# LN(x) of the first layer: from normalized rows kept in DRAM to raw column quarters centred on the fly

## The chip, the cores and the metric

The kernel runs on one core of a Trainium2 chip. That core has a matrix engine (TensorE, PE in the profile), a vector engine (VectorE, DVE), a scalar engine (ScalarE, ACT), a general engine (GpSimd, POOL) and a queue engine that issues most of the transfers (SyncE, SP). Each engine works through its own list of instructions in order and waits for the others by semaphores. The metric is the device time of one execution in microseconds.

## The reference

Four layers act in turn on `x`, an array of 2048 positions by 512 channels. Layers one and three (A) and layers two and four (B) are a LayerNorm, a long causal convolution done by Fourier transforms, and a residual addition.

```python
def _layernorm(x, axis=-1, eps=1e-5):
    m = jnp.mean(x, axis=axis, keepdims=True)
    v = jnp.var(x, axis=axis, keepdims=True)
    return (x - m) / jnp.sqrt(v + eps)
...
    x = A_q
    x = x + _A_ref(_layernorm(x, axis=-1), A_k, A_v, A_shift_k, A_ssm_k, A_ssm_D)
    x = x + _B_ref(_layernorm(x, axis=-1), B_log_A_real, B_A_imag, B_C_real, B_C_imag, B_log_dt, B_D_skip)
...
```

`_A_ref(q, k, v, ...)` returns `q * y`, where `y` comes from `k`, `v` and the filter alone and does not depend on `x`. So the first layer is `x + LN(x) * y`, with `LN(x) = (x - mean) / std`. Both the kernel before and the changed one compute it without the mean, as `x - mean + LN(x) * y`, and keep the mean in a small tile `off` for later. `y` of layer A is stored (`ya_d`) and used again for layer three.

## The kernel before

**Stages.** The program has a planned stage, from about 25 to 550 us of the profiled execution, and then the rest in the order in which it is written: layer two, the update of layer three and layer four. The change touches the planned stage alone.

**What the planned stage holds.** Two generators are recorded side by side. `stream()` makes the taps of layer B's filter: 64 steps, four for each of 16 groups of channels. A step is an angle matmul into the PSUM tile `pa`, a rounding on VectorE (`y`), a second matmul, five sine or absolute-value activations on ScalarE (`ab`, `tt`, `pa`), two products on GpSimd (`xy`) and one on VectorE (`e2`), and 16 small matmuls (`pk`). Every fourth step scales `pk` into `ks`, which goes to DRAM (`kdram`), comes back as `kk`, and is transformed (`pf`, `zk`, `pu`, `pc`) into the filter's spectrum `spec1`. Each of the steps 0, 8, 16 and so on has a block of six exponentials (`m`) ahead of it. I call these 64 steps the taps.

`diagonal()` does layer A: the filter's spectrum (`spectrum_quarter(0, ...)`), the products `kv` of 16 channel groups (`gated`, with operand tile `kvt` and result `u`, eight elementwise operations shared by VectorE and GpSimd), and the convolution for four quarters of 128 channels. The convolution goes by pairs of chunks: `pu` by matmul, a copy `sw` on ScalarE, the products `sw` on GpSimd and `vv` on VectorE with the loaded spectrum `kab`, then the inverse transform `pi` (64 small matmuls a pair), copied back to `zu` by ScalarE, transposed to `w`, and multiplied into `po`. `po` has one PSUM buffer. `finish_a` copies it to `ya` and calls `update_a`, which writes the new `x` of 32 channels.

**Where LN(x) comes from.** `row_stats` loads the 16 blocks of rows of `x` (`xt`, 256 KB each in two transfers) and takes their statistics. `normalizer` turns them into `rs` (1/std), `nm` (minus the mean) and `nb`, at tap 32 (`XN`). `ln_rows(j)` then loads four blocks of rows (`xr`, 1 MB), normalizes each on ScalarE, and writes the result by channel quarter to `ln_d` (16 transfers in all). `load_x(q)` reads a quarter back as `xq`, a single buffer of 1 MB. `update_a` multiplies: `po + std`, then `xq * po`. When a quarter is done it is stored to `x1_d`, and only then can the next quarter be loaded into the buffer.

**What sets the order.** Nothing in the planned stage is issued as it is recorded. `Planner.plan` simulates the recorded operations with a cost for each (`Planner.cost`) and places, again and again, the operation that could start earliest; each engine's list is the result. A transfer is planned to land at the later of 1500 ns after its issue and 1200 ns after a common server, moving 290 bytes a nanosecond, has moved its size. The order so found is fixed: on the chip an engine waits at the head of its list even when later work is ready. SyncE's list is one of these lists: a store that waits for its data holds back the loads behind it. Since all places follow from the costs, a change of cost moves instructions all over the stage.

**Lines.** The profile gives planned instructions the line 319, where the planner emits them, and the others 177; tiles tell them apart.

Of the kernel before, what the change touches and what calls it, by code (L numbers as in the profile page):

```python
# [9 lines left out]
F32 = mybir.dt.float32  # L10
# [10 lines left out]
NQ = 4  # L21
# [87 lines left out]
class Planner:  # L109
# [70 lines left out]
    def cost(self, op):  # L180
        name, a, k = op.calls[0]
        aps = [x for x in list(a) + list(k.values()) if hasattr(x, "tensor")]
        free = lambda x: int(np.prod([c for _, c in x.ap[1:]])) if len(x.ap) > 1 else 1
        n = max(free(x) for x in aps)
        if name == "dma_start":
            size = 4 * n * max(1, aps[0].ap[0][1]) if aps[0].space != DRAM else 4 * int(np.prod([c for _, c in aps[0].ap]))
            return (450 if op.engine == "D" else 600), 1500 + size / 290, size
        big = [x for x in aps[1:] if free(x) > 1]
        psum = [x.space == PSUM for x in big]
        if op.engine == "T":  # L190
            total, each = 0, 0
            for _, b, _ in op.calls:
                d = free(b[2]) * (1 if b[2].dtype == F32R else 4) / 2.4
                area = b[1].ap[0][1] * free(b[1]) / 16384
                total, each = total + d * area, max(each, d)
            return max(total, each), max(total, each) + 230, 0
        if op.engine == "V":
            alone = len(big) == 1 and not psum[0] and name in ("tensor_copy", "tensor_scalar", "tensor_scalar_mul")
            o = 60 + n * (0.52 if alone else 1.06)
            return o, o + 85, len(big) > 1 and not any(psum)  # L200
        if op.engine == "S":
            o = n / 1.2 + (50 if all(psum) else 184)
            if any(hasattr(k.get(x), "tensor") for x in ("scale", "bias")):
                o = n / 1.2 + (186 if name == "activation" and len(big) == 1 else 280)
            return o, o + 105, 0
        o = 100 + 2.2 * n if name.startswith("tensor_tensor") or name in ("tensor_mul", "tensor_add", "tensor_sub") else 100 + 0.9 * n
        return o, o + 50, n > 1
# [123 lines left out]
def kernel(ctx: ExitStack, tc: tile.TileContext, out, x_in, kv_in, ssmk_in, ssmd_in,  # L331
# [13 lines left out]
    ya_d = dram.tile([4, 128, 16, 128], F32, name="ya_d")  # L345
    kv_d = [dram.tile([128, 512], F32, name=f"kv_d{g}") for g in range(16)]

    ln_d = [dram.tile([128, 16, 128], F32, name=f"ln_d{q}") for q in range(NQ)]
    x1_d = [dram.tile([128, 16, 128], F32, name=f"x1_d{q}") for q in range(NQ)]
    rows_d = [dram.tile([NQ, 128, 4, 128], F32, name=f"rows_d{k}") for k in range(2)]  # L350

# [94 lines left out]


    off = cpool.tile([128, 16], F32, name="off")
    std = cpool.tile([128, 16], F32, name="std")
    st = cpool.tile([128, 16, 4, 6], F32, name="st")  # L450
    st_all = lambda t: st[:, t, :, :].rearrange("p q s -> p (q s)")

# [334 lines left out]
    def taps():  # L787
        load_rows(0)
        load_rows(1)

        def exps(gi):
            mags(gi, 0, 2)
            mags(gi, 0, 1)
            mags(gi, 1, 1)

        for n in range(64 + LP + LC):
            gi, k = divmod(n, 4)
            if n < 64:
                if k == 0:
                    if gi > 0 and gi < 15:  # L800
                        load_rows(gi + 1)
                    if EORD == 1:
                        exps(gi)
                    elif EORD == 3 and gi % 2 == 0:
                        exps(gi)
                        exps(gi + 1)
                if n == XN:
                    root = normalizer(0, 16, lambda t: st0[:, t, :])
                    after(root, last_exp[0])
                    last_exp[0] = root  # L810
                    V.reciprocal(std, rs)
                    G.tensor_scalar(off, nm, -1.0, None, op0=ALU.mult)
                angles(gi, k)
                waves(gi, k)
            if 0 <= n - LP < 64:
                products(*divmod(n - LP, 4))
            m = n - LP - LC
            if 0 <= m < 64:
                contract(*divmod(m, 4))
                if m % 16 == 15:  # L820
                    todo.append(spectrum_quarter(1, m // 16, kdram, kp, zlast_k, 1))
            yield
# [12 lines left out]
    with ExitStack() as actx:  # L835
# [29 lines left out]

        KV0 = 1
        KVE = 0b10010110
        def row_stats(t):
            xt = ap.tile([128, 512], F32, name="xt", tag="kk", bufs=NKK)
            by_half(xt, x_in[:, t, :])  # L870
            V.bn_stats(st0[:, t, :], xt)

        def kv_steps():
            for grp in range(KV0, 16):
# [21 lines left out]
            return (lambda: z[0]), [nop] * 7 + [lambda: load(0)] + [nop] * 4 + turns  # L896


        def ln_rows(j):
            xr = ap.tile([128, 4, 512], F32, name="xr", tag="xq", bufs=1)  # L900
            by_half(xr.rearrange("p t c -> p (t c)"), x_in[:, 4 * j:4 * j + 4, :].rearrange("p t c -> p (t c)"))
            for i in range(4):
                t = 4 * j + i
                S.activation(xr[:, i], xr[:, i], AF.Identity, scale=rs[:, t:t + 1], bias=nb[:, t:t + 1])
            for q in range(NQ):
                Q.dma_start(ln_d[q][:, 4 * j:4 * j + 4, :], xr[:, :, 128 * q:128 * q + 128])

        xqs = {}

        def load_x(q):  # L910
            xqs[q] = ap.tile([128, 16, 128], F32, name="xq", tag="xq", bufs=1)
            Q.dma_start(xqs[q], ln_d[q])


        def update_a(q, g, po):
            xs = xqs[q][:, :, 32 * g:32 * g + 32]
            ins = V.tensor_add(po, po, std[:, :, None].to_broadcast([128, 16, 32]))
            V.tensor_mul(xs, xs, po)

        def stats_a(q, c):  # L920
            if 3 <= c < 7:
# [11 lines left out]
        def diagonal():  # L933
            kvs = kv_steps()
            for q in range(NQ):
                for i, _ in enumerate(spectrum_quarter(0, q, ssmk_in, ap, zlast, ZA)):
                    if q == 0 and i == 1:
                        for grp in range(KV0):
                            for _ in gated(grp, 255):
                                pass  # L940
                    if q == 0 and i < 4:
                        Q.dma_start(w2[:, 8 * i:8 * i + 8], w2_in[:, 8 * i:8 * i + 8])
                    if q == 2 and i < 4:
                        ins = Q.dma_start(mm[:, 8 * i:8 * i + 8], mm_in[:, 8 * i:8 * i + 8])
                        after(ins, zlast[0])
                    if q == 3 and i == 0:
                        after(Q.dma_start(w4, w4_in), zlast[0])
                    next(kvs, 0)
                    if q == 3 or q == 2 and i >= 8:
                        row_stats(12 * (q - 2) + i - 8)  # L950
                    yield
            for _ in kvs:
                yield
            for s, _ in enumerate(convolution(0, {"conv": ap}, steps_a, finish_a, lag=LAGA, ahead=AHA, nk=NKA, ns=NSA,
                                              nw=NWA, inplace=True, zlast=zlast, late_step=stats_a), -2 * NCH):
                if s >= LN0 and (s - LN0) % LNS == 0 and s < LN0 + 4 * LNS:
                    ln_rows((s - LN0) // LNS)
                if s >= 0 and s % NCH == LX and s // NCH < NQ:
                    load_x(s // NCH)
                yield  # L960

        LN0, LNS = -8, 3
        LX = 7

        RT = 2
# [247 lines left out]
```

## Time and profile before

| | us |
|---|---|
| median of 3 runs (lowest, highest) | 798.61 (795.02, 799.39) |
| the profiled execution: its time | 799.61 |
| the profiled execution: first to last instruction (span) | 797.6 |
| planned stage, about | 25 to 550 |
| TensorE busy in the span | 551.8 |
| VectorE, ScalarE, GpSimd busy | 516.9, 432.9, 391.1 |
| mean granted TensorE clock | 0.783 of full speed |

The span is read from the trace of one execution; 2.0 us of that execution lie around it. Terms worked out from the trace are taken off or added to the execution's own 799.61 us, which is 1.0 us above the median of the runs. A busy share is an average; which engine ends a wait is read in each stretch, from the chain of waits and from the rows of the timeline.

### The profile page before, as it was taken

To read this page: it belongs to the slowest core of one execution; us is meant where nothing else is said; L and a number is where in the kernel's file an instruction comes from. 1 tells how busy PE (TensorE), PEld (TensorE's weight loads), DVE (VectorE), ACT (ScalarE), POOL (GpSimd) and SP (SyncE) were. 2 spreads that over 40 slices of the span, in tenths; PEclk is the share of its full clock that TensorE was granted. 3 is DMA by queue.
4 is the path that set the end of the run, shared out by engine and by line. 5 is a ranking of instruction groups with operands and counts; after the bars stand their busy time and mean duration, and the time that the engine had idled before them with its cause. 6 is when DMAs were issued, how large, how long until landed. Compare 5 with 4: busy or idle time off the path is not lost.

```text
span 797.6 us, 20671 instructions
## 1 busy us (share of the span) xinstructions
PE 551.8 (69%) x8440; PEld 321.3 (40%) x8440; DVE 516.9 (65%) x931; ACT 432.9 (54%) x800; POOL 391.1 (49%) x362
## 2 busy tenths in 40 slices
PE   1467665576568767697787588763499982669995
PEld 0134333234235333465335246432165560246562
DVE  6545555886864475354567654855368898987773
ACT  4066383284367786873862348813845343847441
POOL 3776768777756172663461315810064441245451
PEclk9995565575855567777659887977789997789998
DMA  8675756464855446758536773646878634047874
GB/s 242 205 177 135 228 168 180 115 174 141 227 149 180 161 129 187 214 174 250 202 98 192 220 271 126 201 139 228 254 261 292 219 133 145 14 134 251 257 223 92
DMA packets 77634, 147.33 MB, mean 185 GB/s; under 512 B 8668, under 2 KB 37732, under 8 KB 74980
## 3 DMA queue, kind: packets, MB, share of 16 engines
q1 hardware_dynamic: 76676, 143.60, 58.4%
q0 software_dynamic: 864, 2.43, 1.0%
q8 instruction: 66, 1.08, 0.6%
q14 instruction: 28, 0.23, 0.1%
HBM read 101.95 MB, written 44.04 MB: 183 GB/s over the span
## 4 chain that ended last, share of the span: by engine, by line
PE 36%; DVE 23%; ACT 17%; issue 9%; DMA 9%; POOL 4%; SPq 1%; DVEq 0%; ACTq 0%; POOLq 0%
PE pf L319 6%; PE pa L319 5%; PE pu L319 5%; PE pk L319 4%; ACT m L319 4%; PE pi L319 4%; PE pi L177 3%; DMA kab<-spec 3%; ACT tt L319 2%; PE pu L177 2%; PE po L319 2%; PE pf L177 2%; DVE zu L177 2%; DVE x L177 2%; DVE w L177 2%
## 5 line engine op out<-in xcount | busy, mean ns | idle before, releaser
L319 POOL TENSOR_TENSOR xy<-tt,m 128x512 f32<-128x512 f32 x128 | 151.6, 1205 | 98.5 <-ACT tt L319 55.2
L177 POOL TENSOR_TENSOR sw<-sw,kab 128x512 f32<-128x512 f32 x64 | 80.7, 1281 | 117.1 <-ACT sw L177 115.5
L319 PE MATMUL pf<-kk,w 64*128 64x512 f32 x128 | 62.7, 955 | 36.6 <-DMA kk<-ssmk_in 19.5
L319 ACT ACTIVATE m<-pm 128x1024 f32<-128x1024 f32 x48 | 47.1, 1023 | 67.6 <-PE pm L319 50.8
L319 PE MATMUL pk<-xy,e 128*32 128x64 f32 x2048 | 57.5, 274 | 17.4 <-POOL xy L319 13.6
L319 DVE STREAM_TRANSPOSE zk<-pf 128x512 f32<-128x512 f32 x64 | 42.1, 693 | 40.3 <-PE pf L319 40.2
L319 DVE TENSOR_TENSOR e<-pa,m 128x512 f32<-128x512 f32 x64 | 43.6, 683 | 35.4 <-ACT pa L319 25.3
L319 ACT ACTIVATE ab<-pa 128x512 f32<-128x512 f32 x64 | 38.2, 597 | 51.2 <-PE pa L319 50.5
L319 POOL TENSOR_TENSOR sw<-sw,kab 128x512 f32<-128x512 f32 x32 | 40.6, 1279 | 51.7 <-ACT sw L319 29.8
L319 PE MATMUL pa<-tt,rw 64*128 64x512 f32 x64 | 42.8, 672 | 32.3 <-DVE e L319 29.7
L177 DVE TENSOR_TENSOR vv<-pu,kab 128x512 f32<-128x512 f32 x64 | 41.2, 679 | 33.8 <-ACT sw L177 30.5
L177 ACT COPY ie<-pi 128x1024 f32<-128x1024 f32 x32 | 32.4, 1013 | 56.0 <-PE pi L177 54.5
L319 PEld LDWEIGHTS pk<-xy,e 128*32 128x32 f32 x2048 | 44.3, 143 | 43.7 <-POOL xy L319 28.1
L319 PE MATMUL pa<-y,minus 128*128 128x512 f32 x64 | 42.6, 671 | 26.2 <-DVE y L319 26.2
L319 DVE TENSOR_SCALAR y<-pa 128x512 fp32r<-128x512 f32 x64 | 43.6, 683 | 25.6 <-PE pa L319 25.5
L319 PE MATMUL pu<-zk,w 64*64 64x128 f32 x1024 | 50.7, 360 | 11.0 <-ACT pc L319 5.2
L319 POOL TENSOR_TENSOR u<-u,tb 128x512 f32<-128x512 f32 x32 | 44.4, 1390 | 23.4 <-DVE tb L319 12.7
L177 PE MATMUL pf<-u,w 64*128 64x512 f32 (+1 forms) x136 | 39.3, 665 | 23.3 <-ACT u L177 15.1
L177 PE MATMUL pi<-vv,mm 64*64 64x128 f32 x1024 | 53.6, 275 | 1.2 <-DVE vv L177 1.1
L177 PE MATMUL pi<-sw,mm 64*64 64x128 f32 x1024 | 52.8, 270 | 0.7 <-issue 0.7
L319 PEld LDWEIGHTS pu<-zk,w 64*64 64x64 f32 x1024 | 42.6, 185 | 26.0 <-issue 12.8
L319 ACT ACTIVATE tt<-pa 128x256 f32<-128x256 f32 x128 | 44.7, 387 | 10.9 <-PE pa L319 7.1
(141 smaller groups left out, 1264.8 us busy)
## 6 DMA issues: line engine op xcount, KB each, us to landing
kab<-spec SPq DMA_DIRECT2D x94, 512.0 KB, 5.4
spec<-pc SPq DMA_DIRECT2D x64, 256.0 KB, 2.2
kvt<-kv_in SPq DMA_DIRECT2D x32, 312.0 KB, 6.0
kk<-ssmk_in SPq DMA_DIRECT2D x32, 128.0 KB, 3.1
kv_d<-u SPq DMA_DIRECT2D x16, 256.0 KB, 4.0
xr<-x_in SPq DMA_DIRECT2D x8, 512.0 KB, 5.1
kdram<-ks SPq DMA_DIRECT2D x64, 64.0 KB, 1.8
kk<-kdram SPq DMA_DIRECT2D x32, 128.0 KB, 2.9
```

The costliest lines, as they stand in the source:

```text
L177: op.ins = getattr(self.engines[key], name)(*a, **k).ins
L319: ins = getattr(self.engines[op.engine], name)(*a, **k).ins
```

## The change

Three things change. `Planner.cost` counts a transfer at the size of its destination. Before, it multiplied the number of destination partitions by the longer of the two sides' free sizes, which counted every half-partition transfer (`by_half`: `kk`, `kvt`, `xr`, `xt`) and every broadcast `kab` load at twice its size.

`row_stats(j)` now loads `xr` (1 MB, four blocks) and takes the statistics from it, four times, in quarter 1 of the filter's spectrum (`LNQ`). `ln_rows` and `ln_d` are gone: no normalized row is written or read back.

`load_x(q)` reads the raw quarter of `x` in four transfers of 32 partitions each (256 KB, in pieces of 512 bytes), and GpSimd subtracts the mean (`off`) in four operations of 128x512. `update_a` becomes `po * rs`, then `(po + 1) * xq`: with `xq = x - mean` this is `x - mean + LN(x) * y` as before. `std` is gone.

```diff
@@ Planner.cost
         if name == "dma_start":
-            size = 4 * n * max(1, aps[0].ap[0][1]) if aps[0].space != DRAM else 4 * int(np.prod([c for _, c in aps[0].ap]))
+            size = 4 * int(np.prod([c for _, c in aps[0].ap]))
@@ taps
-                    V.reciprocal(std, rs)
                     G.tensor_scalar(off, nm, -1.0, None, op0=ALU.mult)
@@
-        def row_stats(t):
-            xt = ap.tile([128, 512], F32, name="xt", tag="kk", bufs=NKK)
-            by_half(xt, x_in[:, t, :])
-            V.bn_stats(st0[:, t, :], xt)
+        def row_stats(j):
+            xr = ap.tile([128, 4, 512], F32, name="xr", tag="xq", bufs=1)
+            by_half(xr.rearrange("p t c -> p (t c)"), x_in[:, 4 * j:4 * j + 4, :].rearrange("p t c -> p (t c)"))
+            for i in range(4):
+                V.bn_stats(st0[:, 4 * j + i, :], xr[:, i])
@@
-        def ln_rows(j):
-            xr = ap.tile([128, 4, 512], F32, name="xr", tag="xq", bufs=1)
-            by_half(xr.rearrange("p t c -> p (t c)"), x_in[:, 4 * j:4 * j + 4, :].rearrange("p t c -> p (t c)"))
-            for i in range(4):
-                t = 4 * j + i
-                S.activation(xr[:, i], xr[:, i], AF.Identity, scale=rs[:, t:t + 1], bias=nb[:, t:t + 1])
-            for q in range(NQ):
-                Q.dma_start(ln_d[q][:, 4 * j:4 * j + 4, :], xr[:, :, 128 * q:128 * q + 128])
@@
         def load_x(q):
             xqs[q] = ap.tile([128, 16, 128], F32, name="xq", tag="xq", bufs=1)
-            Q.dma_start(xqs[q], ln_d[q])
+            rows = x_in[:, :, 128 * q:128 * q + 128].rearrange("(a b n) t c -> a b n t c", a=2, b=2)
+            for b in range(2):
+                for a in range(2):
+                    Q.dma_start(xqs[q][64 * b + a:64 * b + 64:2], rows[a, b])
+            for j in range(4):
+                ts = slice(4 * j, 4 * j + 4)
+                G.tensor_sub(xqs[q][:, ts], xqs[q][:, ts], off[:, ts, None].to_broadcast([128, 4, 128]))
 
         def update_a(q, g, po):
             xs = xqs[q][:, :, 32 * g:32 * g + 32]
-            ins = V.tensor_add(po, po, std[:, :, None].to_broadcast([128, 16, 32]))
-            V.tensor_mul(xs, xs, po)
+            V.tensor_mul(po, po, rs[:, :, None].to_broadcast([128, 16, 32]))
+            V.scalar_tensor_tensor(xs, po, 1.0, xs, op0=ALU.add, op1=ALU.mult)
@@ diagonal
-                    if q == 3 or q == 2 and i >= 8:
-                        row_stats(12 * (q - 2) + i - 8)
+                    if q == LNQ and i % 3 == 0:
+                        row_stats(i // 3)
@@
-                if s >= LN0 and (s - LN0) % LNS == 0 and s < LN0 + 4 * LNS:
-                    ln_rows((s - LN0) // LNS)
                 if s >= 0 and s % NCH == LX and s // NCH < NQ:
                     load_x(s // NCH)
@@
-        LN0, LNS = -8, 3
+        LNQ = 1
         LX = 7
```

Because the costs change, the plan changes everywhere. Three places follow, with the instructions as the two programs list them; the number behind a name tells buffers of one name apart and differs between the programs.

First, SyncE's list around the fourth to seventh load of the convolution's spectrum (`kab`). Before:

```order
L319 DMA kab_771<-spec0_0_57 128x1x1024
L319 DMA raw_936<-rows_d1_107 128x128
L319 DMA kab_773<-spec0_0_57 128x1x1024
L319 DMA kab_790<-spec0_0_57 128x1x1024
L319 DMA ln_d0_98<-xr_734 128x4x128
L319 DMA ln_d1_99<-xr_734 128x4x128
L319 DMA ln_d2_100<-xr_734 128x4x128
L319 DMA ln_d3_101<-xr_734 128x4x128
L319 DMA spec1_1_62<-pc_783 128x512
L319 DMA spec1_1_62<-pc_789 128x512
L319 DMA kab_792<-spec0_0_57 128x1x1024
L319 DMA kab_799<-spec0_0_57 128x1x1024
```

and now:

```order
L319 DMA kab_751<-spec0_0_57 128x1x1024
L319 DMA raw_915<-rows_d1_103 128x128
L319 DMA kab_752<-spec0_0_57 128x1x1024
L319 DMA spec1_1_62<-pc_762 128x512
L319 DMA kab_769<-spec0_0_57 128x1x1024
L319 DMA spec1_1_62<-pc_768 128x512
L319 DMA kab_771<-spec0_0_57 128x1x1024
L319 DMA u_801<-kv_d7_89 128x512
L319 DMA kab_778<-spec0_0_57 128x1x1024
```

The stores of normalized rows, which wait for ScalarE's `xr`, no longer stand between the sixth and the seventh load.

Second, GpSimd's list in the convolution, around the tile `xy` of one tap and the products `sw`. Before:

```order
L319 TENSOR_TENSOR xy_941<-tt0_228,m1_865 128x16x32 x2
L319 TENSOR_TENSOR xy_949<-tt1_229,m1_869 128x16x32 x2
L319 TENSOR_TENSOR xy_981<-tt2_230,m1_871 128x16x32
L319 TENSOR_TENSOR kk_916<-kk_916,dr_879 1x4x8
L319 TENSOR_TENSOR xy_981<-tt2_230,m1_871 128x16x32
```

and now, where the same taps are `xy_920`, `xy_928` and `xy_960`:

```order
L319 TENSOR_TENSOR xy_920<-tt0_223,m1_844 128x16x32 x2
L319 TENSOR_TENSOR sw_912<-sw_912,kab_884 128x512
L319 TENSOR_TENSOR sw_912<-sw_912,kab_904 128x512
L319 TENSOR_TENSOR xy_928<-tt1_224,m1_848 128x16x32
L319 TENSOR_TENSOR xq_908<-xq_908,off_117 128x512 x4
L319 TENSOR_TENSOR xy_928<-tt1_224,m1_848 128x16x32
L319 TENSOR_TENSOR sw_935<-sw_935,kab_909 128x512
L319 TENSOR_TENSOR sw_935<-sw_935,kab_913 128x512
```

The four subtractions of the second quarter stand between the two halves of one tap's `xy`, and the convolution's products stand earlier among the taps. Those of the third quarter stand likewise inside a tap; the first quarter's are spread over a few taps, and the fourth's stand among the last `kk` additions.

Third, ScalarE's list at the end of the planned stage, from the last tap on. Before:

```order
L319 ACTIVATE ab_1101<-pa_1099 128x512
L319 ACTIVATE tt0_228<-pa_1099 128x8x32 x2
L319 ACTIVATE tt0_228<-ab_1101,halfpi_145 128x8x32
L319 ACTIVATE pa_1099<-pa_1099 128x8x32
L319 ACTIVATE pa_1099<-ab_1101,halfpi_145 128x8x32
L319 COPY zu_975<-pi_1092 128x64x16
L319 COPY zu_975<-pi_1104 128x64x16
L319 COPY ya_1108<-po_1107 128x512
```

and now:

```order
L319 COPY zu_954<-pi_1083 128x64x16
L319 ACTIVATE ab_1080<-pa_1078 128x512
L319 ACTIVATE tt0_223<-pa_1078 128x8x32 x2
L319 ACTIVATE tt0_223<-ab_1080,halfpi_140 128x8x32
L319 ACTIVATE pa_1078<-pa_1078 128x8x32
L319 ACTIVATE pa_1078<-ab_1080,halfpi_140 128x8x32
L319 COPY ya_1087<-po_1086 128x512
```

Both last copies of `pi` stood behind the last tap; now both stand ahead of it.

More of the change, by code (lines that the diff above doesn't have):

```diff
@@ L346 @@
     kv_d = [dram.tile([128, 512], F32, name=f"kv_d{g}") for g in range(16)]
-    ln_d = [dram.tile([128, 16, 128], F32, name=f"ln_d{q}") for q in range(NQ)]
     x1_d = [dram.tile([128, 16, 128], F32, name=f"x1_d{q}") for q in range(NQ)]
@@ L448 @@
     off = cpool.tile([128, 16], F32, name="off")
-    std = cpool.tile([128, 16], F32, name="std")
     st = cpool.tile([128, 16, 4, 6], F32, name="st")
```

## Prediction

> **What bounds the kernel now.** I read the summary of the page first, then the busy time by stretches, then the chain of waits in the planned stage, then the timeline of its end.
>
> ```profile
> span 797.6 us, 20671 instructions
> PE 551.8 (69%) x8440; PEld 321.3 (40%) x8440; DVE 516.9 (65%) x931; ACT 432.9 (54%) x800; POOL 391.1 (49%) x362
> ...
> PE 36%; DVE 23%; ACT 17%; issue 9%; DMA 9%; POOL 4%; SPq 1%; DVEq 0%; ACTq 0%; POOLq 0%
> ```
>
> No engine is full. The last line divides the chain that ended last: TensorE has a third, VectorE a quarter, ScalarE a sixth, transfers 9%, GpSimd 4%. So a microsecond taken from one engine is not a microsecond of time; it depends on the stretch.
>
> ```profile
> core 0: us, PE busy (x) PEld busy (x) DVE busy (x) ACT busy (x) POOL busy (x), PEclk, DMA share, GB/s
> 100.00:150.00 50.00, 26.82 (x332) 15.87 (x336) 30.58 (x38) 29.55 (x63) 37.09 (x30) 0.56 0.57 164
> 200.00:250.00 50.00, 33.03 (x425) 18.47 (x425) 34.77 (x58) 25.79 (x53) 33.57 (x30) 0.72 0.64 185
> 300.00:350.00 50.00, 38.47 (x576) 23.85 (x567) 21.56 (x35) 39.44 (x77) 23.81 (x22) 0.69 0.71 204
> 400.00:450.00 50.00, 40.63 (x663) 23.13 (x663) 34.79 (x63) 22.11 (x41) 21.63 (x22) 0.80 0.58 177
> 500.00:550.00 50.00, 35.06 (x594) 20.25 (x594) 36.47 (x77) 21.30 (x42) 18.02 (x18) 0.86 0.55 179
> ```
>
> Up to 250 us GpSimd is the busiest or close to it. From 300 to 350, where `ln_rows` runs, ScalarE is (39 of 50 us) and the transfers are heaviest. From 400 on TensorE and VectorE lead, and GpSimd works under half the time. The change takes ScalarE work and transfers out of the third of these stretches and puts most of its GpSimd work where GpSimd is half idle.
>
> **Part by part.** The sum is made against the profiled execution, 799.6 us.
>
> *(a) The normalization on ScalarE goes.* Sixteen instructions:
>
> ```profile
> L319 ACT ACTIVATE xr<-xr,nb,rs 128x512 f32<-128x512 f32 x16 | 11.7, 801 | 1.6 <-DMA xr<-x_in 1.0 <-DVE nb L319 0.6
> ```
>
> They come in four blocks of 2.9 us. Only one is on the chain:
>
> ```profile
> 335.47 4.61 DMA kab<-spec
> 340.08 0.66 ACT xr L319
> 340.77 2.21 ACT xr L319 x3
> ...
> 347.91 3.48 DMA kab<-spec
> ...
> 359.30 7.42 DMA u<-kv_d
> ```
>
> 0.66 + 2.21 = 2.9. Bounds: 0 (all hidden) and -11.7 (all exposed). I take -2.9, what the chain shows.
>
> *(b) `ln_d`, its queue time and 8 MB of traffic go.* Rows of `x` were read twice (4 + 4 MB), LN(x) written and read (4 + 4); now they are read twice. The chain rows above hold 4.61 + 3.48 + 7.42 = 15.5 us of waits for loads that stand behind `xr` and `ln_d` on SyncE, and SyncE waited for ScalarE's rows:
>
> ```profile
> SPq L319 <- ACT xr L319: 13.8, 3, 6.9
> POOL sw L319 <- DMA kab<-spec: 3.4, 4, 1.3
> ```
>
> The first row: 13.8 us in three waits, at the head of the list, with `kab`, `spec` and `u` behind. In the new list nothing of this kind stands between the `kab` loads. But a load takes its time on a free queue too (the 5.4 us below), so not all of 15.5 can go. Bounds 0 and -15.5; I take about half, -7.
>
> *(c) The end of the stage is shorter.* Rounding of the last tap, then what followed it:
>
> ```profile
> 511.44 0.69 DVE L319 TENSOR_SCALAR y<-pa 128x512 fp32r<-128x512 f32 x1 [0.51 <-PE pa L319]
> 512.61 0.45 PE L319 MATMUL pi<-vv,mm 64*64 64x128 f32 x8
> 514.20 0.34 SPq L319 DMA_DIRECT2D x_d<-xq  x1
> 519.07 0.34 SPq L319 DMA_DIRECT2D xq<-ln_d  x1
> 524.91 2.43 PE L319 MATMUL pf<-kk,w 64*128 64x512 f32 x8
> 531.92 0.69 DVE L319 TENSOR_TENSOR xq<-xq,po 128x512 f32<-128x512 f32 x1
> ...
> 554.01 6.60 DMA x<-x_d
> ```
>
> Two `pi` pairs lie between the tap and the first `pf` (512.61 to 524.91, 12.3 us). In the new lists both precede the last tap; they have to fit into gaps further ahead. Bounds 0 (they displace other work) and -12.3; I take -5.
>
> *(d) Sixteen subtractions on GpSimd come in.* The nearest row, two 128x512 operands on the same engine:
>
> ```profile
> L319 POOL TENSOR_TENSOR sw<-sw,kab 128x512 f32<-128x512 f32 x32 | 40.6, 1279 | 51.7 <-ACT sw L319 29.8 <-DMA spec<-pc 17.7 <-DMA kab<-spec 3.4
> ```
>
> 16 x 1.28 = 20.5 us. Twelve come in three clumps of four, 5.1 us each. Behind a clump wait half an `xy` (then `pk`, `ks`, `kdram`) and the `sw` products. GpSimd was idle 51.7 us ahead of this group alone, so most is covered. Bounds 0 and +20.5; I take one clump exposed, +5.1. Without its cover the whole 20.5 is paid.
>
> *(e) The turnaround of `xq`.* Before, 519.07 to 531.92 lay between the issue of the last quarter's load and its first use, 12.9 us. Now there are four issues on SyncE and then the clump.
>
> ```profile
> kab<-spec SPq DMA_DIRECT2D x94, 512.0 KB, 5.4
> xr<-x_in SPq DMA_DIRECT2D x8, 512.0 KB, 5.1
> ln_d<-xr SPq DMA_DIRECT2D x16, 256.0 KB, 3.9
> x<-x_d SPq DMA_DIRECT2D x4, 1024.0 KB, 10.2
> ...
> L319 SPq DMA_DIRECT2D xr<-x_in x8: 534/554/599, 63.7 to 357.3; - x8
> ```
>
> Issue 4 x 0.55 = 2.2; landing between 3.9 (256 KB in the same 512-byte pieces) and 10.2 (four such megabytes at once); clump 5.1. That is 11.2 to 17.4 against 12.9: 0 to +4.5. I take 0, since one megabyte alone is nearer to the 3.9. Cover: the work of the next pairs between two quarters; if it is gone, every one of three turnarounds pays.
>
> *(f) The start.* The new lists put one statistics instruction of `xr` on VectorE ahead of the first tap's cast, and one more 128x512 operation on GpSimd ahead of the fourth `kk` addition.
>
> ```profile
> L319 DVE BATCH_NORM_STATS2 st<-xt 128x6 f32<-128x512 f32 x16 | 10.8, 675 | 0.0
> ...
> 40.57 0.24 POOL L319 TENSOR_TENSOR kk<-kk,dr 1x32 f32<-1x32 f32 x1
> ...
> 45.07 0.48 DVE L319 CAST rw<-raw 128x256 fp32r<-128x256 f32 x2
> 47.11 1.29 DVE L319 TENSOR_SCALAR y<-pa 128x512 fp32r<-128x512 f32 x2 [1.55 <-PE pa L319]
> ```
>
> 0.7 + 1.3 = 2.0. If `xr` (5.1 us to land) is late the first tap is too: bounds 0 and +5.1. I take +2. The other statistics only move earlier, from a stretch where VectorE was busy 35 of 50 us to one with 31: 0.
>
> *(g) `update_a`.* One instruction for one, the second with a constant:
>
> ```profile
> L177 DVE SCALAR_TENSOR_TENSOR x<-x,nm,ut 128x512 f32<-128x512 f32 x16 | 11.6, 732 | 0.8 <-ACT ut L177 0.8
> L319 DVE TENSOR_TENSOR xq<-xq,po 128x512 f32<-128x512 f32 x16 | 10.8, 673 | 0.2
> ```
>
> 16 x (0.732 - 0.673) = +0.9, taken whole, because the next `po` waits for it.
>
> Sum: -2.9 - 7 - 5 + 5.1 + 0 + 2 + 0.9 = -6.9; 799.6 becomes 792.7, and the median of the runs, 798.6, becomes 791.7: **792 us**. What the new order does elsewhere has no price here; it is in the rivals.
>
> **The rivals.** *Larger gain.* The waits of (b) and (c) go whole: -2.9 - 15.5 - 12.3 + 5.1 + 2 + 0.9 = -22.7, 776 us. For it: SyncE loses its only stores that wait for ScalarE in the convolution. Against: the freed time must be usable by TensorE, which is 77% busy there.
>
> *Slower: the plan now believes that loads land too early.* By the formula of `cost` a `kab` load was planned at 450 + 1048576 / 290 + 1200 ns = 5.3 us; now at 450 + 524288 / 290 + 1200 = 3.5. The trace has 5.4. The double counting was near the truth, and the right size is 1.9 us short for each of 32 loads, 62 us in all. Place: `vv` and `sw` reach the head of VectorE and GpSimd too early, and `y`, `e2` and `xy` of the taps queue behind. One in four exposed is +15.5: -6.9 + 15.5 = +8.6, 807 us. It decides from the point where the waits of `sw` and `vv` for `kab` pass some 10 us. For it: the same holds for `kk` and `kvt`. Against: the 3.4 us above are all that GpSimd waited for `kab`, and SyncE is freer.
>
> *Slower: the clumps are exposed.* All of 20.5 in (d) and 4.5 in (e): -6.9 + 15.4 + 4.5 = +13.0, 812 us. Against: GpSimd's idle time.
>
> *No difference: the clumps empty TensorE.* The same pair of 64 matmuls costs
>
> ```profile
> 471.64 2.01 PE pi L319 x64
> ...
> 488.19 3.64 PE pi L319 x64
> ```
>
> depending on the clock it is granted (0.56 on average from 100 to 150 us, 0.86 from 500 to 550). If each of three clumps leaves TensorE without work long enough that the next pair falls to the slower row, 3 x 1.63 = +4.9 comes on top: -2.0, 796.6 us. The Trainium skill, "TensorE: Matmul & The Clock Gate", Part 1, says that an idle window of about 3.4 us halves the clock until work has been sustained again; a clump of 5.1 us is longer than that, so by the page this would be the outcome wherever nothing else feeds TensorE. The two rows above, nearly two to one, agree with its two states; the lengths of the windows no row here shows.
>
> That the change does not do what it says I leave out: the `ln_d` rows are gone from the new lists.
>
> **How the numbers follow.** Forecast (792, its own range 785 to 797) 0.42; larger gain 0.22; no difference 0.08; too early loads 0.18; exposed clumps 0.10. The range runs from 776 to 811: half of the larger gain and half of the exposed clumps lie outside, which leaves out 0.16. A measurement of this kernel can tell about 0.5% (4 us) from no change. Faster by more: 0.39 of the forecast's 0.42, and the 0.22, gives 0.61. Within: 0.03 + 0.08 = 0.11. Slower: 0.18 + 0.10 = 0.28.
>
> **What would show it.** (a, b) No wait of SyncE for ScalarE's `xr`, and fewer microseconds of `DMA kab` and `DMA u` in the chain between 330 and 370. (c) Less than the 42.6 us from the last `y` (511.4) to the first load of the next stage (554.0). (d) GpSimd busy about 411 us, `xq` rows near 1.28 us, and little waiting of `pk` for `xy`. (e) Little GpSimd waiting for `xq` loads. (f) The first `y` at about 49 instead of 47.1 us. The forecast is wrong if `sw`, `vv` or `kk` wait over 10 us more for loads, if the taps take longer with the same work, or if the stage ends where it did with the waits moved.

## The result, and the profile after

The changed kernel takes 756.18 us (median of four runs, 752.62 to 758.29); the kernel before took 798.42 us in the same series (795.02 to 799.39). The ratio is 0.947, with a 95% interval of 0.943 to 0.952. The prediction was 792 us with a range of 776 to 811: the sign was right, the size was not, and the time lies below the range.

The head of the page of the changed kernel:

```profile
span 756.2 us, 20631 instructions
PE 527.1 (70%) x8440; PEld 306.3 (40%) x8440; DVE 513.7 (68%) x930; ACT 421.1 (56%) x784; POOL 407.6 (54%) x378
```

ScalarE lost 11.8 us and GpSimd gained 16.5, about what the instructions added and removed come to. Neither explains 41 us of span. TensorE ran the same 8440 matmuls in 24.7 us less, at a mean granted clock of 0.814 instead of 0.783. The five stretches shown before (the columns are the same):

```profile
100.00:150.00 50.00, 31.96 (x362) 17.35 (x358) 33.92 (x51) 29.30 (x63) 33.77 (x28) 0.60 0.58 162
200.00:250.00 50.00, 39.57 (x491) 23.18 (x491) 30.89 (x39) 28.25 (x57) 36.23 (x33) 0.61 0.56 168
300.00:350.00 50.00, 40.32 (x815) 27.45 (x811) 27.57 (x43) 36.57 (x70) 31.60 (x29) 0.86 0.53 164
400.00:450.00 50.00, 37.75 (x585) 21.99 (x578) 28.75 (x55) 31.11 (x56) 24.69 (x24) 0.77 0.64 189
500.00:550.00 50.00, 26.82 (x420) 15.93 (x420) 27.52 (x76) 28.08 (x58) 10.04 (x8) 0.74 0.73 242
```

From 200 to 250 us and from 300 to 350 TensorE now runs 39.6 and 40.3 of 50 us (before 33.0 and 38.5), in the latter with 815 matmuls instead of 576 at a clock of 0.86 instead of 0.69. The last stretch is for the most part another part of the program: the planned stage ends 14 us into it. The clock alone does not make the time: over whole spans it was 0.826 in a kernel of 780 us below and 0.811 in one of 760.

**Where the time came from.** The first load of layer two's `x` marks the end of the planned stage. It was issued at 554.01 us before, and now, in the timeline of the changed kernel:

```profile
476.67 0.67 DVE L319 TENSOR_SCALAR y<-pa 128x512 fp32r<-128x512 f32 x1
...
506.57 0.69 DVE L319 SCALAR_TENSOR_TENSOR xq<-po,xq 128x512 f32<-128x512 f32 x1
507.30 3.19 DVE L319 BATCH_NORM_STATS2 st<-xq 128x6 f32<-128x128 f32 x16
507.78 0.61 SPq L319 DMA_DIRECT2D x_d<-xq  x1
513.58 2.62 SPq L177 DMA_DIRECT2D x<-x_d  x2
```

So 40.4 us of the 41.4 us of span are gained before this point, and the rest of the program is unchanged (243.6 us before, 242.6 now). The stretch from the last `y` to this load went from 42.6 to 36.9 us. The other 34.8 us came earlier, while the taps still ran. The largest piece is one pause between two taps. Before (`y` is the rounding of a tap):

```profile
436.85 0.68 DVE L319 TENSOR_SCALAR y<-pa 128x512 fp32r<-128x512 f32 x1
486.46 0.69 DVE L319 TENSOR_SCALAR y<-pa 128x512 fp32r<-128x512 f32 x1
```

and in the changed kernel, for the same pair of taps:

```profile
417.37 0.69 DVE L319 TENSOR_SCALAR y<-pa 128x512 fp32r<-128x512 f32 x1 [0.34 <-PE pa L319]
445.22 0.69 DVE L319 TENSOR_SCALAR y<-pa 128x512 fp32r<-128x512 f32 x1
```

Before, no tap was rounded for 49.6 us; now the pause is 27.9. The chain of waits of the kernel before shows what filled it (start, length, what):

```profile
430.62 3.45 PE pi L319 x64
...
442.59 4.28 DMA spec<-pc
446.87 0.68 DVE po L319
447.57 0.70 DVE xq L319
...
458.75 1.98 PE po L319 x4
...
464.84 2.01 PE pi L319 x64
...
471.64 2.01 PE pi L319 x64
...
476.00 5.74 ACT m L319 x6
```

It is layer A's convolution, pair after pair, done here with no tap rounded beside it. The width of this pause says where the plan has put that work; it is not by itself the loss, as the experiments show. The same shift is visible at its beginning. SyncE's first load of `kab` before and now:

```profile
267.31 0.54 SPq L319 DMA_DIRECT2D kab<-spec  x1
```

```profile
224.00 0.54 SPq L319 DMA_DIRECT2D kab<-spec  x1
```

The convolution starts 43 us earlier. This alone is not the gain either: with the raw read alone (below) the first `kab` was issued at 233.4 us, and the kernel gained 7 us.

### The profile page after: what moved, and what is told of

It is laid out like the page before. It is cut to its first block, busy times and chain, and to the rows that moved or that the text cites. A ratio compares the mean times of both kernels' runs of the same rounds, so it can differ in the third digit from the quotient of the medians.

```text
span 756.2 us, 20631 instructions
## 1 busy us (share of the span) xinstructions
PE 527.1 (70%) x8440; PEld 306.3 (40%) x8440; DVE 513.7 (68%) x930; ACT 421.1 (56%) x784; POOL 407.6 (54%) x378
## 3 DMA queue, kind: packets, MB, share of 16 engines
q8 instruction: 66, 1.08, 0.6%
## 5 line engine op out<-in xcount | busy, mean ns | idle before, releaser
L319 PE MATMUL pf<-kk,w 64*128 64x512 f32 x128 | 57.3, 945 | 34.3 <-POOL kk L319 18.5
L319 DVE TENSOR_TENSOR e<-pa,m 128x512 f32<-128x512 f32 x64 | 43.7, 682 | 38.8 <-ACT pa L319 15.9
L319 PE MATMUL pa<-tt,rw 64*128 64x512 f32 x64 | 41.4, 650 | 35.1 <-DVE e L319 34.1
L319 DVE TENSOR_SCALAR y<-pa 128x512 fp32r<-128x512 f32 x64 | 43.5, 682 | 23.7 <-PE pa L319 22.5
L319 POOL TENSOR_TENSOR u<-u,tb 128x512 f32<-128x512 f32 x32 | 44.3, 1388 | 24.3 <-DVE u L319 11.5
L177 PE MATMUL pf<-u,w 64*128 64x512 f32 (+1 forms) x136 | 39.6, 676 | 24.7 <-ACT u L177 17.0
L319 PE MATMUL pa<-y,minus 128*128 128x512 f32 x64 | 40.3, 629 | 23.1 <-DVE y L319 22.9
L319 PE MATMUL pu<-zk,w 64*64 64x128 f32 x1024 | 48.6, 347 | 3.8 <-ACT m L319 1.5
L177 ACT COPY sw<-pu 128x1024 f32<-128x1024 f32 x32 | 32.3, 1014 | 29.8 <-PE pu L177 29.8
L319 PEld LDWEIGHTS pu<-zk,w 64*64 64x64 f32 x1024 | 40.3, 177 | 17.6 <-issue 10.1
```

Source lines behind the costliest of these rows:

```text
L177: op.ins = getattr(self.engines[key], name)(*a, **k).ins
L319: ins = getattr(self.engines[op.engine], name)(*a, **k).ins
```

## The experiments

All kernels were compared with the kernel before on the same chip in the same series. Its median was between 796.9 and 801.0 us in these series, and times below are medians.

### One part of the change at a time

*True sizes alone*, in the kernel before:

```diff
-            size = 4 * n * max(1, aps[0].ap[0][1]) if aps[0].space != DRAM else 4 * int(np.prod([c for _, c in aps[0].ap]))
+            size = 4 * int(np.prod([c for _, c in aps[0].ap]))
```

> The kernel before with the true transfer sizes in the plan alone; LN(x) still goes through DRAM. Theory 'late rows' (the first quarter of LN(x) was ready only after 381 us, 90 us behind its statistics, and held up the convolution): little changes, 785 to 803 us, and the first xq multiplication stays later than 385 us. Theory 'sizes' (the gain is the better order that the true sizes give): most of the 42 us, 756 to 772 us. Theory 'scatter' (any new plan differs by chance): anywhere within 15 us of 798.

*The raw read alone*: the changed kernel with the line above undone.

> The changed kernel with the old, partly doubled sizes in the plan. 'Late rows': most of the gain stays, 750 to 770 us. 'Sizes': most is lost, 785 to 800 us. 'Scatter': neither, in between, about 775.

*Statistics early*: the kernel before with the new `row_stats(j)` in quarter 1, `ln_rows` and `ln_d` kept; and the same with the normalizer at tap 16.

```diff
-                    if q == 3 or q == 2 and i >= 8:
-                        row_stats(12 * (q - 2) + i - 8)
+                    if q == 1 and i % 3 == 0:
+                        row_stats(i // 3)
```

> The kernel before with the row statistics taken from 1 MB blocks in quarter 1 of the filter spectrum, as the change does, but with the normalizer still at tap 32, and LN(x) still through DRAM with its own loads. 'Late rows': the four cycles still start at tap 32, so 785 to 803 us. 'Sizes': the same, 785 to 803. A third theory, that the statistics' place in VectorE's busy stretch was the cost: below 780 us.

```diff
-    XN = 32
+    XN = 16
```

> As the run with early statistics, but with the normalizer at tap 16 instead of 32: LN(x) still goes through DRAM with old sizes, only some 80 us earlier. 'Late rows': the first xq is ready before the first po needs it, and most of the gain appears without the raw load, 755 to 775 us. 'Sizes', and the theory that it is the work and traffic taken out that counts: no gain, 785 to 803 us.

Measured:

| kernel | us | ratio to before (95%) |
|---|---|---|
| true sizes alone | 774.1 | 0.970 (0.965 to 0.976) |
| raw read alone | 790.8 | 0.992 (0.988 to 0.996) |
| early statistics | 803.8 | 1.008 (1.003 to 1.012) |
| early statistics, normalizer at tap 16 | 789.4 | 0.990 (0.986 to 0.993) |
| both parts: the changed kernel | 756.2 | 0.947 (0.943 to 0.952) |

The raw read alone gives 7.0 us, true sizes alone 23.7, both together 42. True sizes alone lie 2 us above the 756 to 772 that the theory of sizes asked for, but 9 us and more below what the other theories allowed. Late rows of `x` cannot be the main cause. With true sizes alone the first update of `xq` still came at 388 us (403 before, 355 in the changed kernel), and the kernel gained 24 us; with the normalizer at tap 16 it came at 377 us, and the kernel gained 8, where the theory of late rows asked for 23 or more. Early statistics alone lost 6 us, 1 us beyond both expectations. In its trace the same pause was wider still:

```profile
413.36 0.69 DVE L319 TENSOR_SCALAR y<-pa 128x512 fp32r<-128x512 f32 x1
488.85 0.69 DVE L319 TENSOR_SCALAR y<-pa 128x512 fp32r<-128x512 f32 x1
```

75.5 us without a tap. But the tap ahead of it came 23.5 us earlier than in the kernel before, and the one behind it 2.4 us later. With true sizes alone the pause was 45.8 us (419.58 to 465.40), nearly as wide as before, and the kernel was 24 us faster. So the pause shows the order that the plan chose, not what that order costs, and I turned to the plan.

### What the plan believed

The planner's times follow from the program's text alone, and can be worked out with its own arithmetic. Adding up the sizes that it counts in the planned stage gives 139.0 MB in the kernel before and 86.8 MB in the changed one. Its one transfer server moves 290 bytes per ns, so it was booked for 479 of 510 planned us before, and is booked for 299 of 422 now. A booked server has a queue, and the queue is in the planned landing. The median landings over all loads of a kind (in the plan, of an even number of loads, the upper of the two middle ones):

| load | planned before | measured before | planned now | measured now |
|---|---|---|---|---|
| `kab` | 12.7 us | 5.4 | 4.5 | 4.8 |
| `kvt` | 9.7 | 6.0 | 4.6 | 5.2 |
| `spec` | 7.2 | 2.2 | 3.0 | 3.0 |
| `u` from DRAM | 10.4 | 6.6 | 3.6 | 3.1 |

The measured numbers are the medians to landing in the view of DMA issues; for the changed kernel:

```profile
kab<-spec SPq DMA_DIRECT2D x94, 512.0 KB, 4.8
spec<-pc SPq DMA_DIRECT2D x64, 256.0 KB, 3.0
kvt<-kv_in SPq DMA_DIRECT2D x32, 312.0 KB, 5.2
...
u<-kv_d SPq DMA_DIRECT2D x16, 256.0 KB, 3.1
```

Of the 94 `kab` loads the plan holds 32; the other 62 belong to later stages. The 32 alone landed in 5.6 us before and 4.4 now (medians), which changes nothing here.

Before, the plan held these loads to be 1.6 to 3.3 times as slow as they are, and put everything that needs one late in the lists. The pause at taps 58 to 59 is in the plan itself: 53.1 us planned before and 49.6 measured, 21.6 planned now and 27.9 measured. With early statistics it was 70.9 planned and 75.5 measured.

### Moving the belief without the sizes

If landings that are planned too long are the cause, then the rate in the plan must do the same as the sizes; and if a plan simply lands at random within some 15 us, it must not. Two kernels before and two changed kernels with nothing but another rate:

```diff
-                server = max(server, t + o) + extra / 290
+                server = max(server, t + o) + extra / 435
```

> Nothing of the kernel before changes but the rate by which its plan counts transfers, 290 to 435 bytes per ns (the counted 139 MB of the planned stage fall from 479 to 319 us of a single server; the 24 MB too many stay counted). Overbooked queue (the plan holds work back because its one transfer server is booked for most of the stage): 772 to 782 us, most of what true sizes alone gave (774.1). Scatter (any new order of this plan lands somewhere within some 15 us, with no trend): anything from 783 to 812.

> As the run with 435, with 580 bytes per ns: 240 us of the server booked. Overbooked queue: no slower than the run with 435, 768 to 780 us. Scatter: no relation to the run with 435; above 785 us in at least one of the two.

> The changed kernel with 200 bytes per ns in place of 290 in its plan: its 86.8 MB count as 434 us of the server, nearly as booked as before (479 us). Overbooked queue: slower than 756.2, between 765 and 790 us, with the first xq after 360 us. Scatter: no trend; 756 plus or minus 15.

> The changed kernel with 435 bytes per ns: 200 us of the server booked in place of 299. Overbooked queue: little is left to gain, 748 to 760 us. Scatter: 756 plus or minus 15, so above 762 or below 745 would speak for it.

Measured: the kernel before with 435, 760.1 us (0.953, 0.944 to 0.963); with 580, 794.2 (0.996, 0.993 to 0.999). The changed kernel with 200, 781.8 (0.980, 0.974 to 0.986); with 435, 779.8 (0.978, 0.971 to 0.985).

The first is the strongest single result. One number in the planner, with the wrong sizes, `ln_d` and ScalarE's normalization all kept, gives 36.8 us of the gain. That is 12 us better than the range I had given. (By the planner's sums, 139.0 MB against 95.2 with true sizes, 43.8 MB too many stayed counted there, not 24.) The third takes most of it away again. Its first update of `xq` came at 356 us, though, not after 360 as expected. Its pause is back (416.23 to 459.92 us between the roundings, 43.7 us; its plan has 40.0).

The second and the fourth missed what I expected of an overbooked server: a still emptier one was no longer better, but 34 and 24 us worse. These two outcomes are what the theory of scatter had named as its sign, so an empty queue alone does not explain the times. Their pause at tap 58 is short (27.1 and 25.9 us); they lose elsewhere, the changed kernel with 435 at the start: it was 14 us behind the changed kernel at the third tap and 23 behind at the 21st. In the stretch from 25 to 75 us, the changed kernel with 435 and then the changed kernel as it is:

```profile
25.00:75.00 50.00, 15.16 (x91) 7.46 (x91) 25.20 (x49) 12.77 (x21) 24.38 (x22) 0.82 0.76 184
```

```profile
25.00:75.00 50.00, 27.16 (x259) 14.99 (x259) 29.80 (x49) 22.27 (x46) 33.77 (x29) 0.93 0.88 216
```

91 matmuls instead of 259. The timeline of the kernel with 435 says what VectorE did meanwhile (start, length, and in brackets the wait ahead and its releaser):

```profile
45.98 2.47 DVE L319 BATCH_NORM_STATS2 st<-xr 128x6 f32<-128x512 f32 x4 [14.06 <-DMA xr<-x_in]
49.22 0.49 DVE L319 CAST rw<-raw 128x256 fp32r<-128x256 f32 x2
...
56.46 2.47 DVE L319 BATCH_NORM_STATS2 st<-xr 128x6 f32<-128x512 f32 x4 [2.62 <-DMA xr<-x_in]
...
67.23 1.29 DVE L319 BATCH_NORM_STATS2 st<-xr 128x6 f32<-128x512 f32 x2 [5.64 <-DMA xr<-x_in]
...
74.32 0.69 DVE L319 TENSOR_SCALAR y<-pa 128x512 fp32r<-128x512 f32 x1 [0.21 <-PE pa L319]
```

Three times in this stretch it stood at the head of its list for a load of `xr`, 14.06 us the first time. The plan had `xr` land in 3.6 us (median) and put the statistics where it would be there. Behind them stand the cast `rw` and the taps. Its waits from 25 to 125 us (engine, line, waited for: total, times, longest) show who is held:

```profile
DVE st L319 <- DMA xr<-x_in: 25.1, 4, 14.1
...
PE pa L319 <- DVE rw L319: 22.7, 1, 22.7
```

The third tap was rounded at 74.3 us instead of 60.4 in the changed kernel, where the longest such wait was 1.97 us:

```profile
46.29 0.69 DVE L319 BATCH_NORM_STATS2 st<-xr 128x6 f32<-128x512 f32 x1 [1.97 <-DMA xr<-x_in]
```

The kernel before with 580 lost in the same way, but on other loads and over a longer stretch. Up to 125 us GpSimd stood 14.3 us for one load of `kvt` and VectorE 9.8 us for one of `raw`; it was 17 us behind the kernel with 435 at the 13th tap, and 31 behind at the 37th. This is the rival of loads planned too early, in kernels other than the changed one.

### Giving the right landing back

So a plan can err on both sides. If the measured landing is what counts, then the two kernels with too short landings must recover when each landing is counted 1500 ns longer, which changes no size and no rate, and small steps from the changed kernel must cost little.

```diff
-                end[n] = max(t + o + 1500, server + 1200)
+                end[n] = max(t + o + 3000, server + 2700)
```

> The changed kernel with 435 bytes per ns in its plan (779.8 us so far) and every transfer counted as landing 1500 ns later, which brings the planned landings back to those measured (median kab load 2.9 to 4.4 us planned, 4.6 measured; kvt 2.8 to 4.3). Landing theory (the plan is good when its landings are those of the chip; longer ones make it hold work back, shorter ones put readers ahead of their data in the engines' queues): 754 to 768 us. Scatter (each order lands at random within some 20 us): no recovery is owed, 756 to 795 alike.

> The kernel before with 580 bytes per ns (794.2 us so far) and every transfer counted as landing 1500 ns later (kab median 4.0 to 5.4 us planned, 4.9 measured; kk 2.1 to 3.6, kvt 3.4 to 4.9). Landing theory: 758 to 776 us, near the 760 of the run with 435, where the planned landings were also near those measured. Scatter: no recovery is owed, 760 to 800 alike.

> The changed kernel with 330 bytes per ns in place of 290: planned landings a little short (kab 3.6 us, kvt 3.5). Landing theory: between the runs with 290 (756.2) and 435 (779.8), 755 to 770 us. Scatter: 756 to 795 alike.

> The changed kernel with every transfer counted as landing 500 ns later (kab 5.1 us, kvt 4.8, kk 3.1, spec 3.5: as near to those measured as in the changed kernel itself). Landing theory: 751 to 764 us. Scatter: 756 to 795 alike; above 772 would speak for it.

Measured, in this order: 767.2 us (0.960, 0.955 to 0.965), 765.9 (0.960, 0.954 to 0.966), 766.4 (0.961, 0.955 to 0.966), 757.5 (0.949, 0.944 to 0.954). All four lie where the landing theory put them. The wide ranges of scatter hold them too; what speaks against scatter is that all four came out on the right side together. 779.8 fell to 767.2, and 794.2 to 765.9.

### What is left for the raw read, and the subtractions

Sizes and raw read give 30.7 us apart and 42 together. If the missing 11 us are the transfers of `ln_d` that the kernel before still has in its plan (8.4 MB), they should come with a slightly higher rate. The second edit moves the 16 subtractions to VectorE.

> The kernel before with true sizes (774.1 us so far) and 320 bytes per ns in its plan, so that its 95.2 MB take 298 us of the server as the changed kernel's 86.8 MB do at 290. If the missing 11 us are the LN transfers that the plan still counts (landing theory): 758 to 767 us, and reading x raw is then worth some 4 to 8 us by itself. If they are a gain of the raw read that only shows with true sizes: 770 to 778 us, nothing changed.

```diff
-                G.tensor_sub(xqs[q][:, ts], xqs[q][:, ts], off[:, ts, None].to_broadcast([128, 4, 128]))
+                V.tensor_sub(xqs[q][:, ts], xqs[q][:, ts], off[:, ts, None].to_broadcast([128, 4, 128]))
```

> The changed kernel with its 16 subtractions on VectorE. If GpSimd was charged rightly (the 16 are 16 to 20 us of GpSimd at some 1.0 to 1.3 us each, a quarter of it on the path): 748 to 755 us. If the subtractions are hidden on GpSimd: 754 to 764 us, no gain, since VectorE then carries some 11 us more.

The first gave 783.1 us (0.980, 0.975 to 0.985), outside both expectations and 9 us slower than without the new rate. It landed on the short side again: `kvt` planned 3.6 us and measured 5.7, `xr` planned 6.6 and measured 8.9. Yet the changed kernel with 330 plans `kvt` just as short (3.5, measured 5.4) and took 766.4. So the landings do not order neighbouring plans. Two more kernels settle whether the theory or this setting failed: the kernel before with true sizes and the two settings that were good for the changed one (435 with 1500 ns more, 290 with 500 ns more).

> The kernel before with true sizes, 435 bytes per ns and landings 1500 ns later (planned: kab 4.4 us, kvt 4.3, kk 3.5, xt 3.5, all near those measured). Landing theory: 757 to 770 us, as the changed kernel with the same setting (767.2). Order scatter of some 10 us on top of it, or the raw read needed for the gain: 770 to 785.

> The kernel before with true sizes, 290 bytes per ns and landings 500 ns later (kab 5.6 us planned, kvt 4.8, kk 4.0, xr 7.6, ln_d 5.5). Landing theory: no slower than the same without the 500 ns (774.1): 760 to 774 us. Scatter: 774 plus or minus 10, above 777 as well as below.

Measured: 763.4 us (0.958, 0.953 to 0.963) and 767.2 (0.961, 0.955 to 0.967), both as the landing theory had it; the first is below what scatter allowed, the second is not. The table puts the runs side by side. "Slip" is the time of layer two's first load minus the planned length of the stage (both kinds of start offset are in it, so only differences count).

| kernel | plan's `kab`, `kvt` landing | planned length | first load | slip | us |
|---|---|---|---|---|---|
| before | 12.7, 9.7 | 510 | 554 | 44 | 798 |
| early statistics, tap 16 | 12.7, 9.8 | 509 | 543 | 34 | 789 |
| early statistics | 12.2, 9.8 | 518 | 556 | 39 | 804 |
| raw read alone | 11.5, 9.8 | 488 | 548 | 60 | 791 |
| changed, 200 | 9.6, 8.6 | 483 | 536 | 53 | 782 |
| true sizes alone | 6.2, 4.3 | 435 | 529 | 94 | 774 |
| before, 435 | 6.4, 4.4 | 428 | 512 | 84 | 760 |
| true sizes, 500 ns more | 5.6, 4.8 | 435 | 521 | 85 | 767 |
| before, 580, 1500 ns more | 5.4, 4.9 | 428 | 513 | 85 | 766 |
| changed, 500 ns more | 5.0, 4.8 | 425 | 511 | 86 | 757 |
| changed, subtractions on VectorE | 4.6, 4.6 | 419 | 510 | 91 | 753 |
| changed | 4.5, 4.6 | 422 | 514 | 92 | 756 |
| true sizes, 435, 1500 ns more | 4.4, 4.3 | 424 | 510 | 86 | 763 |
| changed, 435, 1500 ns more | 4.4, 4.3 | 426 | 518 | 92 | 767 |
| changed, 330 | 3.6, 3.5 | 420 | 513 | 94 | 766 |
| true sizes, 320 | 4.5, 3.6 | 424 | 540 | 116 | 783 |
| before, 580 | 4.0, 3.4 | 420 | 549 | 129 | 794 |
| changed, 435 | 2.9, 2.8 | 413 | 535 | 122 | 780 |

The first five plans are long, and the chip comes within 34 to 60 us of them; their times are 782 to 804. Between them and the last three lie ten plans of 419 to 435 us, with times of 753 to 774. So plans that overrate the landings are set apart from the others. The last three, with 780 to 794, are hardly shorter (413 to 424 us), but the chip misses them by 116 to 129. Here the two medians do not set the groups apart: the changed kernel with 330 has shorter ones than the kernel with true sizes and 320, and is 17 us faster. Size, rate and added time move the landings of all transfers at once; which of them matter was not separated.

What the raw read is worth by itself depends on the setting beside it: 790.8 against 797.8 with the old sizes (7 us), 756.2 against 774.1 with true ones (18), 757.5 against 767.2 with 500 ns more (10), 767.2 against 763.4 with 435 and 1500 ns more (4 us lost). Some 8 us on average, then, from a loss of 4 to a gain of 18, which does not set it apart from the spread between plans. That spread is the part that I could not explain; the 11 us that neither part gives alone are within it.

The subtractions on VectorE gave 753.3 us (0.944, 0.940 to 0.949). The time lies where I expected it if a quarter of the subtractions is on the path, but the interval overlaps that of the changed kernel, so a gain of 3 us is not shown. GpSimd's group in the changed kernel, and VectorE's in this one:

```profile
L319 POOL TENSOR_TENSOR xq<-xq,off 128x512 f32<-128x512 f32 x16 | 16.2, 1038 | 3.4 <-DMA xq<-x_in 3.4
```

```profile
L319 DVE TENSOR_TENSOR xq<-xq,off 128x512 f32<-128x512 f32 x16 | 11.3, 766 | 1.7 <-DMA kdram<-ks 1.7
```

Here 16.2 us on one engine were traded for 11.3 on another. In this kernel the pause between the two taps is 13.1 us instead of 27.9:

```profile
433.20 0.68 DVE L319 TENSOR_SCALAR y<-pa 128x512 fp32r<-128x512 f32 x1
446.31 0.69 DVE L319 TENSOR_SCALAR y<-pa 128x512 fp32r<-128x512 f32 x1
```

Yet the second of them was rounded 1 us later than in the changed kernel (445.22). A narrower pause is worth nothing when the tap ahead of it comes later.

## Why the prediction was wrong

**The step that failed** is the sentence after the sum, that what the new order does elsewhere has no price. The new order was the larger part of the change: true sizes alone are 23.7 us, another rate alone 36.8. The rivals did not hold it either, because of one piece of arithmetic in the rival of loads planned too early. There I worked out the planned landing of `kab` for an idle server, 5.3 us before and 3.5 now, and concluded that the double counting was near the truth. The server was not idle but booked for 94% of the planned stage, and the plan's own landing, with its queue, was 12.7 us before and 4.5 now, against 5.4 and 4.8 measured. The planned landing was not near the truth but more than twice it, and putting the size right was a gain where that rival had a loss. The rival's mechanism is real: it appeared as soon as the plan was made quicker still.

**(a), (b)** belong to the raw read. That alone changed the time by -7.0 us, as the whole sum had it (-6.9), but not by the sum's terms: in that kernel the stretch from the last `y` (491.7) to layer two's first load (547.6) grew to 55.9 us, and the taps ended 20 us earlier. The agreement is luck within the spread of the plans. The wait of SyncE for ScalarE's `xr` is gone, as (b) asked, but it was 13.8 us. SyncE's longest sums in the planned stage fell too, from 67.2 and 45.8 us, with no edit to what they wait for; they now are

```profile
SPq L319 <- ACT pc L319: 51.0, 30, 8.0
SPq L319 <- PE pf L319: 35.8, 15, 6.7
```

The chain between 330 and 370 us, which I had named as a test, cannot be read in the changed kernel: its chain does not reach back that far.

**(c) The end of the stage** has the right size in the changed kernel: -5.7 us measured, -5 predicted. But this stretch, 42.6 us before, took from 25.9 to 55.9 us in the other kernels of the experiments, and 34.2 in the kernel before with another rate alone. So the agreement does not show that the term is right.

**(d)** GpSimd is busy 407.6 us (411 predicted), and a subtraction takes 1.04 us instead of 1.28. One clump in the open was the value taken. The trace shows one for which TensorE stood long, the fourth. Ahead of it GpSimd waited 2.46 us for the load, and behind it TensorE stood, in the timeline of the changed kernel:

```profile
481.78 1.08 PE L319 MATMUL po<-w,w 128*64 128x512 f32 x4
...
492.43 1.97 PE L319 MATMUL po<-w,w 128*64 128x512 f32 x4 [5.86 <-DVE xq L319]
...
497.92 1.97 PE L319 MATMUL po<-w,w 128*64 128x512 f32 x4 [1.51 <-DVE xq L319]
```

The same four matmuls take 1.08 us ahead of the wait and 1.97 behind it. This is the mechanism of the rival that I called no difference. The Trainium skill, "TensorE: Matmul & The Clock Gate", Part 1, has the clock halved after an idle window of about 3.4 us; the wait of 5.86 us is longer, and the two rows agree. A long wait is not the only way there: four such matmuls also took 1.98 us at 406.77, 4.5 us behind the clump of the second quarter, where TensorE had not waited longer than 1.09 us since the fast ones at 398.01 (1.08 us). Whether that clump brought it about was not tested.

**(e)** No cost, as taken (its upper sum is 17.5, not 17.4): in the whole stage GpSimd waited little for `xq`, `kk` and `kab`:

```profile
POOL xq L319 <- DMA xq<-x_in: 3.4, 3, 2.5
...
POOL kk L319 <- DMA kk<-kdram: 1.7, 2, 1.2
POOL sw L319 <- DMA kab<-spec: 1.5, 1, 1.5
```

The rival of early loads asked for more than 10 us of such waits and is out for the changed kernel; that of exposed clumps would have had all of them in the open, and TensorE stood long for one.

**(f)** Right in size: +2.0 predicted, +2.45 measured. But with true sizes alone, where no statistics stand there, the first tap came at 49.58 us, as late; so the term's reason is not shown. In the changed kernel it is rounded at

```profile
49.56 1.29 DVE L319 TENSOR_SCALAR y<-pa 128x512 fp32r<-128x512 f32 x2 [0.36 <-PE pa L319]
```

**(g)** Cheaper than taken: the new second instruction takes 0.677 us, the old one took 0.673.

```profile
L319 DVE SCALAR_TENSOR_TENSOR xq<-po,xq 128x512 f32<-128x512 f32 x16 | 10.8, 677 | 3.3 <-POOL xq L319 3.2
```

**The rival of a larger gain** had the time nearest to the result (776), but for reasons that were not the cause. It was the sum of the same terms at their bounds, and the cause was in none of them.

## What to carry to other kernels

Where a program orders its own work by a table of costs, a change of that table is a change of its own. Run the table's arithmetic, compare the landings it plans, queue included, with the landings that the profile shows, and expect a gain from a plan that was too pessimistic and a loss from one that is too optimistic. In this kernel an error to the long side went with late bunches of work that the plan itself contains, but the width of a bunch did not measure the loss. An error to the short side showed as engines standing at the head of their lists for a load; the median landings alone did not tell which plans suffer from it. With the changed kernel's work, four plans near the measured landings took 756 to 767 us; with the old work, five took 760 to 774. So this kernel scatters by 11 to 14 us between plans that look equally good, and no edit of it that moves the order can be priced finer than that.

## What the hardware showed

A subtraction of 128x512 on GpSimd with a broadcast second operand took 1.04 us, where the product of two full tiles took 1.28; on VectorE the same subtraction took 0.77.

Loads of one kind and size landed in very different times with another order around them: `xr`, 512 KB, in 5.9 us (median) in the changed kernel and 8.9 in the kernel before with true sizes and 320; `kvt`, 312 KB, in 5.2 us in the changed kernel and 8.8 with 435 in its plan. What beside them lengthens a landing was not tried.
